# First half of the keys' weights moved to another transfer queue, three short warm-up matmuls removed

## The chip, the cores and the metric

The kernel runs on 1 core of one Trainium2 chip. The time is in device microseconds, from launch to end on that core; lower is better. Before the change it is 173.73 us, the median of 3 runs (173.68 to 174.08).

## The reference: what is computed

A layer norm feeds two branches, whose results are added to the input. Branch A is linear attention: queries, keys and values from one weight matrix, a learned feature map for each of 32 heads (a 16 x 16 matrix, then softmax of the result and of its negative), and a projection. Branch B is a dense layer of width 1792 with the mish activation. All tensors are bf16; S = 2048 tokens, D = 512.

```python
def _A_ref(x, wqkv, w_phi, wo):
    qkv = (x @ wqkv).reshape(B, S, 3, H, Dh).transpose(2, 0, 3, 1, 4)
    q, k, v = qkv[0], qkv[1], qkv[2]
    pq = einsum("bhsd,hdf->bhsf", q, w_phi); pk = einsum("bhsd,hdf->bhsf", k, w_phi)
    phi_q = concatenate([softmax(pq), softmax(-pq)], -1)
    phi_k = concatenate([softmax(pk), softmax(-pk)], -1)
    kv = einsum("bhsf,bhsd->bhfd", phi_k, v); z = einsum("bhsf->bhf", phi_k)
    num = einsum("bhqf,bhfd->bhqd", phi_q, kv)
    den = einsum("bhqf,bhf->bhq", phi_q, z)[..., None] + 1e-6
    return (num / den).transpose(0, 2, 1, 3).reshape(B, S, D) @ wo

def _B_ref(x, w1, b1, w2):
    h = einsum("bsd,df->bsf", x, w1) + b1
    act = h * tanh(softplus(h))
    return einsum("bsf,fd->bsd", act, w2)

xn = layernorm(x)
return x + _A_ref(xn, A_wqkv, A_w_phi, A_wo) + _B_ref(xn, B_w1, B_b1, B_w2)
```

## The kernel before

Tokens are worked on in 16 tiles of 128, four tiles to a group, with the 512 input features in four chunks of 128 rows (kt = 0 to 3). Everything stays in on-chip memory between its load and its last use. The order of the work on every engine is written out by hand: STEPS (line 24) is a list of short step names, each of which issues its instructions when its turn comes, and each engine executes its own instructions in the order in which they were issued. Nothing is reordered later.

The start is what matters here. The feature map's matrix w_phi is folded into the keys' weights once, so that one product of the tokens with the folded weights gives the logits of the keys. For that, the keys' weights (a 512 x 512 block of wqkv) are needed turned. Rows 256 to 511 (kt = 2, 3) are turned by a transposing transfer straight into the tile wT (line 483). Rows 0 to 255 (kt = 0, 1) are loaded as they are into the tile wkp (line 482) and turned on TensorE. The steps in question:

- Warm-ups (line 519): WARM = 9 matmuls of 512 columns and SHORT = 3 of 128 columns on constants, ahead of all else on TensorE. Their results are not used.
- PB (line 537): TensorE transposes the bias b1, loaded by ScalarE's first transfer.
- LS, RS, AZ (lines 165, 171 and 557, 176): layer norm of the first two token tiles: statistics on VectorE, root on GpSimd for tile 0 and on ScalarE for tile 1, application on VectorE.
- TW 0, TW 1 (line 576): TensorE turns rows 0 to 127 and rows 128 to 255 of the keys' weights, four matmuls each. TP 0, TP 1 (line 569): it turns the two token tiles.
- TK 0, TK 1 (line 582): ScalarE copies the turned weights from PSUM into wT.
- WB (line 528): VectorE spreads w_phi (tile wsrc, ScalarE's second transfer, line 488) into the block-diagonal Wbd.
- F0 and FD (lines 151, 160): fold of one chunk on TensorE, and the copy of the folded chunk back into wkp, on ScalarE for chunks 0, 2 and 3, on VectorE for chunk 1. TC (line 588): the copy of a turned token tile.
- LP (line 204): the first logits, eight matmuls. V, H, L (lines 189, 223): values, hidden layer and further logits, which then fill TensorE. M (line 234) is the mish on ScalarE.

Transfers are issued by SyncE, in this order: token tiles 0 and 1, wkp, the transposing load into wT, token tiles 2 and 3, the values' weights wv, the first half of w1, token tiles 4 to 7, the second half of w1, and later ones. ScalarE issues two: b1, then w_phi, both before its first activation table is loaded (line 495). Transfers use eight completion counters in turn; a transfer is issued only when the one that used its counter before has landed.

Of the kernel before, what the change touches and what calls it, by code (L numbers as in the profile page):

```python
# [19 lines left out]

WARM, SHORT = 9, 3
STEPS = """
KM; LS 0; RS 0 p; LS 1; RS 1 a; DX 2; PB @0; AZ 0; AZ 1; TW 0 @1; TW 1 @2; TP 0 @3; TP 1 @4; TK 0 a;
TK 1 a; WB; F0 0 @5; FD 0 a; F0 1 @1; TC 0 v; F0 2 @2; F0 3 @3; FD 2 a; TC 1 v; FD 1 v; FD 3 a; LP i
# [36 lines left out]
def kernel(  # L63
# [12 lines left out]
    nc = tc.nc  # L76
    P = 128
    S, D, NH, DH, F = 2048, 512, 32, 16, 1792
# [10 lines left out]
    wqkv_v = A_wqkv.rearrange("(kt p) c -> p kt c", p=P)  # L89
# [29 lines left out]
    wkp = wts.tile([P, KT, D], BF16, name="wkp")  # L119
# [359 lines left out]


    wT_of = {0: lnp.tile([P, 4, 512], BF16, name="wT", tag="xn")}
    nc.sync.dma_start(wkp[:, 0:2, :], wqkv_v[:, 0:2, D : 2 * D])
    nc.sync.dma_start_transpose(
        out=wT_of[0][:, :, 2 * P : 4 * P], in_=A_wqkv[2 * P : 4 * P, D : 2 * D]
    )
    nc.scalar.dma_start(b1b[:], b1_v[:, :])
    with nc.allow_non_contiguous_dma(reason="tiny w_phi load"):
        nc.scalar.dma_start(wsrc[:], wphi_v)
    nc.sync.dma_start(x_sb[:, 2:4, :], x_v[:, 2:4, :])
    nc.sync.dma_start(wv[:], wqkv_v[:, :, 2 * D : 3 * D])  # L490
    nc.sync.dma_start(w1_sb[:, :, 0 : 7 * P], w1_v[:, :, 0 : 7 * P])
# [189 lines left out]
```

## Time and profile before

| | before |
|---|---|
| median of the runs | 173.73 us |
| the profiled execution | 173.71 us |
| its span, first to last instruction | 172.0 us |
| TensorE (PE) busy | 168.0 us, 98% |
| VectorE (DVE) busy | 143.9 us, 84% |
| ScalarE (ACT) busy | 123.8 us, 72% |
| GpSimd (POOL) busy | 7.8 us, 5% |
| read from HBM, written | 7.10 MB, 2.10 MB |

The profile is that of one execution. Times in it count from the start of the span. PEld is TensorE's weight load, SP is SyncE; a name with a q (SPq, ACTq, PEq) is that engine's sequencer, which issues transfers. In a timeline, a row gives start, duration, engine, line, operation, what is written from what, how many, and in brackets the idle time ahead of it with what ended that. A row of merged instructions gives the whole stretch. The chain of work that ended last is followed back from the last instruction, at each step to what released it. A DMA share over 100% means that packets of one engine overlapped. Line numbers are those of the kernel before.

### The profile page before, as it was taken

The page shows a single profiled execution, that of the slowest core. Times are in us where ns is not written, and L with a number is a line of the kernel's source. Part 1 is how long each engine was busy: PE and PEld are TensorE (multiplying, and loading weights), DVE is VectorE, ACT ScalarE, POOL GpSimd, SP SyncE. Part 2 cuts the span into 40 slices and gives each one's busy share as a digit, 9 for nine tenths or more (in the row PEclk, how much of TensorE's full clock was granted, in tenths as well). Part 3 has the DMA queues.
Part 4 walks back from the last instruction along what each step waited for, and adds up shares of the span by engine and source line. Part 5 has one row for each costly group of instructions (what it writes and reads, how often), then busy time and mean ns, then how long its engine had stood idle before and what let it go on. Part 6 is the DMA issues. An engine that isn't in the chain of part 4 may idle for free.

```text
span 172.0 us, 2735 instructions
## 1 busy us (share of the span) xinstructions
PE 168.0 (98%) x1047; PEld 82.6 (48%) x1047; DVE 143.9 (84%) x223; ACT 123.8 (72%) x199; POOL 7.8 (5%) x23
## 2 busy tenths in 40 slices
PE   8899999999999999999999999999999999999993
PEld 2554444444454544454445644544444444554452
DVE  3869998999599999969989999799799998884333
ACT  2778899997999989889978989977282792432200
POOL 4123002300000000000000000000000000000000
PEclk9999999999999999999999999999999999999999
DMA  4997299589000000000000194309335618668941
GB/s 124 303 370 248 54 255 347 99 162 228 21 0 0 0 4 0 0 0 0 4 0 0 36 113 99 61 9 150 90 97 116 153 52 197 146 134 216 110 131 61
DMA packets 44185, 18.02 MB, mean 105 GB/s; under 512 B 35980, under 2 KB 44172, under 8 KB 44172
## 3 DMA queue, kind: packets, MB, share of 16 engines
q1 hardware_dynamic: 43472, 17.73, 43.9%
q8 instruction: 8, 0.13, 0.4%
q10 hardware_dynamic: 700, 0.12, 0.4%
q14 instruction: 5, 0.04, 0.1%
HBM read 7.10 MB, written 2.10 MB: 53 GB/s over the span
## 4 chain that ended last, share of the span: by engine, by line
PE 95%; DMA 2%; SPq 0%; ACT 0%; issue 0%; DVE 0%
PE po L457 28%; PE ph L223 28%; PE pl L189 14%; PE po L464 8%; PE pv L189 8%; PE pnd L412 2%; PE pkv L381 2%; DMA wkp<-in_A_wqkv_dram 2%; PE pl L204 1%; PE pfold L151 1%; PE pwide L189 1%; SPq L478 0%; PE ptr L569 0%; PE ptw L576 0%; ACT wT L582 0%
## 5 line engine op out<-in xcount | busy, mean ns | idle before, releaser
L457 PE MATMUL po<-w_sb,acts 128*128 128x512 bf16 (+2 forms) x238 | 50.8, 366 | 0.0
L223 PE MATMUL ph<-xnT,w_sb 128*128 128x512 bf16 x224 | 49.8, 379 | 0.0
L234 ACT ACTIVATE acts<-ph,b1f 128x512 bf16<-128x512 f32 x56 | 36.3, 701 | 4.2 <-PE ph L223 4.0
L300 DVE TENSOR_REDUCE s<-e 128x128 f32<-128x2048 bf16 x16 | 36.1, 2276 | 0.5 <-ACT e L283 0.5
L223 PEld LDWEIGHTS <-w_sb 128*128 128x128 bf16 x224 | 21.7, 98 | 25.7
L457 PEld LDWEIGHTS <-acts 128*128 128x128 bf16 x238 | 22.1, 98 | 23.6
L283 ACT ACTIVATE e<-e 128x2048 bf16<-128x2048 bf16 x16 | 30.5, 1919 | 0.0
L189 PEld LDWEIGHTS <-xnT 128*128 128x128 bf16 x184 | 17.5, 98 | 19.6
L471 DVE TENSOR_TENSOR x_sb<-po,x_sb 128x512 bf16<-128x512 f32 (+2 forms) x17 | 11.0, 656 | 8.4 <-PE po L464 8.4
L464 PE MATMUL po<-wqk,xnT 128*128 128x512 bf16 (+2 forms) x68 | 15.6, 366 | 0.0
L189 PE MATMUL pv<-wv,xnT 128*128 128x512 bf16 x64 | 15.6, 379 | 0.0
L189 PE MATMUL pl<-wqk,xnT 128*128 128x512 bf16 x64 | 15.4, 379 | 0.0
L427 ACT COPY ds<-pnd 128x32 f32<-128x32 f32 x16 | 2.9, 182 | 16.5 <-PE pnd L412 16.5
L247 ACT CAST p_sb<-pl 128x512 bf16<-128x512 f32 x21 | 12.2, 594 | 3.6 <-PE pl L189 3.4
L139 ACT ACT_TABLE_LOAD x10 | 12.8, 1283 | 0.2
L258 DVE TENSOR_TENSOR m<-m 128x512 bf16<-128x512 bf16 (+1 forms) x32 | 11.5, 359 | 1.1
L189 PE MATMUL pl<-wkp,xnT 128*128 128x512 bf16 x48 | 11.7, 379 | 0.0
L267 DVE TENSOR_TENSOR e<-p_sb,m 128x2048 bf16<-128x2048 bf16 x8 | 9.8, 1226 | 1.8 <-PE pkv L381 1.5
L258 DVE TENSOR_TENSOR m<-p_sb 128x1024 bf16<-128x1024 bf16 x16 | 10.9, 681 | 0.0
L165 DVE BATCH_NORM_STATS2 stats<-x_sb 128x6 f32<-128x512 bf16 x16 | 10.1, 677 | 0.9 <-DMA x_sb<-in_A_x_dram 0.9
L267 DVE TENSOR_TENSOR e<-m,p_sb 128x2048 bf16<-128x2048 bf16 x8 | 9.8, 1225 | 0.3
L334 DVE TENSOR_TENSOR e<-e,r 128x2048 bf16<-128x2048 bf16 x8 | 9.6, 1216 | 0.5 <-ACT r L309 0.5
(68 smaller groups left out, 133.9 us busy)
## 6 DMA issues: line engine op xcount, KB each, us to landing
w_sb<-in_B_w_dram SPq DMA_DIRECT2D x4, 896.0 KB, 7.8
out_dram<-x_sb SPq DMA_DIRECT2D x15, 128.0 KB, 1.8
x_sb<-in_A_x_dram SPq DMA_DIRECT2D x3, 512.0 KB, 7.5
wv<-in_A_wqkv_dram SPq DMA_DIRECT2D x1, 512.0 KB, 4.6
wqk<-in_A_wo_dram SPq DMA_DIRECT2D x1, 512.0 KB, 4.9
x_sb<-in_A_x_dram SPq DMA_DIRECT2D x2, 128.0 KB, 2.1
wkp<-in_A_wqkv_dram SPq DMA_DIRECT2D x1, 256.0 KB, 3.6
x_sb<-in_A_x_dram SPq DMA_DIRECT2D x1, 256.0 KB, 3.6
```

What stands on the lines that cost most here:

```text
L139: nc.scalar.preload_act_table_set(name)
L189: nc.tensor.matmul(pp, lhsT=xnT[:, t, kt, :], rhs=w[:, kt, :], start=(kt == 0), stop=(kt == KT - 1),)
L223: nc.tensor.matmul(ph_of[u][:], lhsT=w1_sb[:, kt, f * P : (f + 1) * P], rhs=xnT[:, g * TPG : (g + 1) * TPG, kt, :], start=(kt == 0), stop= ...
L234: nc.scalar.activation(acts[:, f, g * 512 : (g + 1) * 512], ph_of.pop(u)[:], ACT.Mish, bias=b1f[:, f : f + 1])
L247: copy(p_of[s][:, i, :], pl_of.pop((s, i)))
L258: nc.vector.tensor_tensor(out=m[:], in0=src[:, :, 0:half], in1=src[:, :, half : 2 * half], op=op)
L267: nc.vector.tensor_tensor(out=e_of[s][:].rearrange("p t j l c -> p (t j) l c")[:, :, pl, :].rearrange("p t (c e o) -> p t c e o", e=8, o=2 ...
L283: nc.scalar.activation(v, v, ACT.Exp)
L300: nc.vector.reduce_sum(t[:], pair(s, k).rearrange("p t j l (c e) -> p (t j l c) e", e=16), axis=AX.X)
L457: nc.tensor.matmul(po_of[t, c.stop][:, c], lhsT=acts[:, f, t * P : (t + 1) * P], rhs=w2_sb[:, f, c], start=(f == 0), stop=False,)
L464: nc.tensor.matmul(po_of[t, c.stop][:, c], lhsT=oT_of[t // 2][:, t % 2 * 4 + j, :], rhs=wo_sb[:, j, c], start=False, stop=(j == 3),)
L471: nc.vector.tensor_tensor(out=y, in0=po_of.pop((t, c.stop))[:, c], in1=y, op=ALU.add)
```

## The change

The load of the keys' weights is split by rows. Rows 128 to 255 (kt = 1) stay with SyncE, at the old place as its third transfer. Rows 0 to 127 (kt = 0) become ScalarE's third transfer, behind b1 and w_phi and ahead of its table load. The three short warm-ups are removed, the nine long ones stay. The steps and their order are the same on every engine, TW 0 ahead of TW 1 included. One transfer more means that from there on each transfer uses the next of the eight completion counters.

```diff
-WARM, SHORT = 9, 3
+WARM, SHORT = 9, 0
...
     wT_of = {0: lnp.tile([P, 4, 512], BF16, name="wT", tag="xn")}
-    nc.sync.dma_start(wkp[:, 0:2, :], wqkv_v[:, 0:2, D : 2 * D])
+    nc.sync.dma_start(wkp[:, 1, :], wqkv_v[:, 1, D : 2 * D])
     nc.sync.dma_start_transpose(
         out=wT_of[0][:, :, 2 * P : 4 * P], in_=A_wqkv[2 * P : 4 * P, D : 2 * D]
     )
     nc.scalar.dma_start(b1b[:], b1_v[:, :])
     with nc.allow_non_contiguous_dma(reason="tiny w_phi load"):
         nc.scalar.dma_start(wsrc[:], wphi_v)
+    nc.scalar.dma_start(wkp[:, 0, :], wqkv_v[:, 0, D : 2 * D])
     nc.sync.dma_start(x_sb[:, 2:4, :], x_v[:, 2:4, :])
```

## The prediction

> **What bounds the kernel now.** I read the busy table first, then the chain of work that ended last, then the first ten microseconds by engine and by queue. The page's busy table and its shares of the chain say which engine sets the end.
>
> ```profile
> PE 168.0 (98%) x1047; PEld 82.6 (48%) x1047; DVE 143.9 (84%) x223; ACT 123.8 (72%) x199; POOL 7.8 (5%) x23
> PE 95%; DMA 2%; SPq 0%; ACT 0%; issue 0%; DVE 0%
> ```
>
> TensorE is busy in 168.0 of 172.0 us. Only 4 us of the span can hold a stall of its own, and the chain's one transfer with 2% is the keys' weights, which the change touches. The stretches show that TensorE doesn't pause again once it has started.
>
> ```profile
> core 0: us, PE busy (x) PEld busy (x) DVE busy (x) ACT busy (x) POOL busy (x), PEclk, DMA share, GB/s
> 9.40:40.00 30.60, 30.60 (x149) 14.13 (x148) 27.53 (x65) 27.97 (x40) 5.26 (x8) 1.00 0.79 213
> ...
> 160.00:168.00 8.00, 8.00 (x43) 3.98 (x42) 2.98 (x5) 0.94 (x3) 0.00 (x0) 1.00 0.44 115
> ```
>
> From 9.4 us to 168 us PE's busy time equals the length of each stretch (the rows left out do too). Whatever moves the work at 9.4 us therefore moves the end by as much; nothing behind it can take up a delay. The question is what the change does before 9.4 us, and the chain of waits of that window answers what sets it.
>
> ```profile
> 1.72 3.59 DMA wkp<-in_A_wqkv_dram
> 5.31 0.05 issue
> 5.36 0.62 PE ptw L576 x8
> 5.98 0.24 PE ptr L569 x4
> 6.22 0.06 issue
> 6.28 0.60 ACT wT L582
> 6.88 0.05 issue
> 6.92 0.84 PE pfold L151 x12
> 7.77 1.79 PE pl L204 x8
> 9.56 0.65 PE pv L189 x3
> ```
>
> Columns are start, duration, what. The load of the first 256 rows of the keys' weights (SyncE's third transfer) lands at 5.31 us. The TW matmuls that turn them start 0.05 us later, ScalarE copies the result (TK), the folds follow, then the first logits, then the full stream. So the first TW at 5.36 us is the hinge: **d**, its shift, is the shift of the end.
>
> **The change part by part.** SyncE's load keeps only rows 128 to 255 (kt = 1); rows 0 to 127 (kt = 0) go out on ScalarE's queue as its third transfer. TensorE's order is kept, so TW 0, which reads kt = 0, still comes first: it waits for the new transfer alone, and behind it in TensorE's queue stand TW 1, the transposes of the tokens and every fold. The half that now lands early gains nothing by itself. These are the issues and ScalarE's work around them.
>
> ```profile
> 1.47 0.41 ACTq L488 DMA_DIRECT2D wsrc<-in_A_w_phi_dram  x1
> 1.91 1.28 ACT L495 ACT_TABLE_LOAD   x1 [1.91 <-issue]
> 4.75 0.29 ACT L557 ACTIVATE rstd<-mv,eps 128x1 f32<-128x1 f32 x1 [1.55 <-DVE mv L167]
> 5.08 0.20 ACT L558 ACTIVATE rstd<-rstd 128x1 f32<-128x1 f32 x1
> 5.79 1.07 ACT L582 CAST wT<-ptw 128x512 bf16<-128x512 f32 x2 [0.51 <-PE ptw L576]
> ```
>
> The added issue on ScalarE takes about 0.41 us, as the one before it does. It runs from 1.9 to 2.3 us and pushes the table load's end from 3.19 to 3.6 us. That is hidden: the next ScalarE work starts at 4.75 us, for another reason, and 1.1 us of idle time is left. Now the landing. The page's table of issues gives the prices, from issue to landing.
>
> ```profile
> x_sb<-in_A_x_dram SPq DMA_DIRECT2D x2, 128.0 KB, 2.1
> wkp<-in_A_wqkv_dram SPq DMA_DIRECT2D x1, 256.0 KB, 3.6
> wsrc<-in_A_w_phi_dram ACTq DMA_DIRECT2D x1, 16.0 KB, 4.0
> ```
>
> A 128 KB load with nothing ahead of it took 2.1 us, so the lower bound of the landing is 1.9 + 2.1 = 4.0 us. But the new load stands behind w_phi, 16 KB in many tiny pieces, which took 4.0 us and landed at 1.47 + 4.0 = 5.47 us, later than the keys' weights. What the queues moved in four stretches (2.8 to 3.4, 3.4 to 4.8, 4.8 to 5.0, 5.0 to 5.3 us; packets, MB, share of 16 engines; q1 is SyncE's queue, q10 ScalarE's) says why.
>
> ```profile
> q1 hardware_dynamic: 44, 0.04, 38.2%
> q10 hardware_dynamic: 169, 0.01, 14.8%
> ...
> DMA packets 965, 0.35 MB, mean 250 GB/s; under 512 B 736, under 2 KB 965, under 8 KB 965
> q1 hardware_dynamic: 657, 0.34, 106.8%
> q10 hardware_dynamic: 308, 0.01, 12.3%
> ...
> q10 hardware_dynamic: 11, 0.00, 3.1%
> ...
> DMA packets 249, 0.06 MB, mean 212 GB/s; under 512 B 249, under 2 KB 249, under 8 KB 249
> q1 hardware_dynamic: 249, 0.06, 103.2%
> ```
>
> ScalarE's queue still moves its last tiny packets at 4.8 to 5.0 us and none after: w_phi is trickled out between SyncE's larger packets. If the queue keeps its order, the new 128 KB begin on each engine when w_phi's packets there are through. At the 250 GB/s of the second stretch 128 KB take 0.52 us: unrelieved, it lands at 5.47 + 0.52 = 5.99 us. Two corrections. SyncE's queue holds 128 KB less ahead of w_phi's later packets, a relief of at most 0.52 us; 308 of ScalarE's packets in these stretches, out of 488, ran beside the keys' load, so I take 308/488 x 0.52 = 0.33 us. Against that, the transposing load of the other weights' rows comes up in SyncE's queue (the 249 packets under 512 B) and takes turns with the new packets. That costs between nothing and 0.52 us (its 256 KB against the new 128 KB, at most byte for byte); I take 0.17 us, about a third, since its packets are the smaller. The landing is then 5.99 - 0.33 + 0.17 = 5.83 us, d = 5.83 - 5.31 = +0.52 us. The bounds behind w_phi are 5.47 us (full relief, no turns) and 6.51 us (no relief, full turns): d = +0.16 to +1.2 us.
>
> The Trainium skill says in DMA: Bandwidth & Descriptors, section Queues, rings and completion order, that each engine consumes a queue's descriptors in ring order, and in the section Issuing engines are not separate DMA queues, that transfers of several issuers interleave on the same 16 engines. Both speak against a gain here; the rows above agree on the interleaving (both queues move in the same stretches), and no row of before shows two large transfers behind each other on ScalarE's queue.
>
> The nine long **warm-ups** stay, the three short ones go.
>
> ```profile
> L514 PEld LDWEIGHTS <-const-bfloat16-1.0 x12: 99/147/147, 0.8 to 4.5; 128*128 128x128 bf16 x12
> L514 PE MATMUL warm<-const-bfloat16-1.0 x12: 221/631/631, 0.8 to 4.6; 128*128 128x512 bf16 x9, 128*128 128x128 bf16 x3
> L576 PE MATMUL ptw<-ident,wkp x8: 219/219/230, 5.4 to 5.8; 128*128 128x128 bf16 x8
> ...
> 0.83 4.00 PE L514 MATMUL warm<-const-bfloat16-1.0 128*128 128x512 bf16 x12 [0.83 <-PEq L665]
> ...
> 4.49 0.34 PE L514 MATMUL warm<-const-bfloat16-1.0 128*128 128x128 bf16 x3
> 4.76 0.18 PE L537 MATMUL pb<-ident,b1b 14*128 14x14 bf16 x1
> ```
>
> Here TensorE's weight loads go from 147 to 99 ns and its short matmuls run at 221 ns, like the TW matmuls behind them (219), so its clock was up before the short ones were through; a long one takes 631 ns before that. The short ones free some 0.2 us ahead of TensorE's wait at 5.36 us, so their removal is worth nothing at the end, and lengthens the pause in front of TW from 0.4 to about 1.2 us.
>
> Also moved: the transfers share eight completion counters in turn, so each issue waits for the transfer eight places before it. With one more transfer, the load of tokens 4 to 7 waits for w_phi instead of the first tokens.
>
> ```profile
> 5.23 0.51 SPq L492 DMA_DIRECT2D x_sb<-in_A_x_dram  x1
> 12.76 2.47 DVE L165 BATCH_NORM_STATS2 stats<-x_sb 128x6 f32<-128x512 bf16 x4 [0.57 <-DMA x_sb<-in_A_x_dram]
> ```
>
> It would issue at 5.5 instead of 5.23 us, in a queue that at 5.0 to 5.3 us is full (103.2% above), with the values' and the hidden layer's weights ahead of it; what hides it is that backlog. Without it VectorE's statistics at 12.76 us would be 0.3 us later, and VectorE isn't on the chain. Cost: nothing. Nothing of it passes POOL's queue.
>
> **Sum**: 0.52 (TW 0 waits for its load) + 0 (issue) + 0 (warm-ups) + 0 (counters). The profiled execution took 173.71 us, span 172.0 and 1.71 around it; the median shown is 173.73. 173.71 + 0.52 = 174.23 us.
>
> **Rivals.** *The relief wins.* Each queue carries 128 KB, both are fed at the same time, and the new load lands at or before 5.3 us. For it: between 2.8 and 3.4 us SyncE's queue used 38.2% of the engines, so there was room. Against it: w_phi's last packets at 4.8 us. The gain has an end: ScalarE's copy at 5.79 us can't start before ScalarE's own root ends (5.08 + 0.20 = 5.28 us), so at most 0.5 us; 0.45 with a hand-over of 0.05. That gives 173.26 to 173.71 us; say 173.5. It is the case that is not slower.
>
> *The transposing load goes first.* If its 256 KB are served wholly ahead of the new load, the latter lands with or after 6.5 us, d = +1.2 us: 174.9 us. It decides once SyncE's queue gets more than a byte for each of ScalarE's. For it: 249 packets in 0.3 us at 103.2% while ScalarE's had ended. Against it: in the second stretch 308 tiny packets came through beside 657.
>
> *TensorE drops back to half clock* in the longer pause. The long warm-ups ran from 0.83 to 4.49 us, 3.66 us, until the clock was up; the same again at half speed costs half of that, 1.8 us: 175.5 us. Against it: the present pause of 0.4 us does no harm, and 1.2 us isn't far from it. In the Trainium skill, TensorE: Matmul & The Clock Gate, section Part 1: The HAM clock gate, half clock returns only after an idle window of about 3.4 us; by that rule this rival costs nothing. No run here shows a pause of that length.
>
> *The change doesn't do what it says*: both halves land together as before, d = 0, 173.71 us; that is the upper end of the first rival.
>
> **How the numbers follow.** Forecast 0.60; relief or no change 0.24; transposing load first 0.10; half clock 0.06. A time within 0.3%, 0.52 us, is about what a measurement of this kernel can't tell from no change, and the forecast lies on that edge (174.25 us). More of its bounds lies above the edge than below, so of its 0.60 I give 0.34 to slower and 0.26 to same: slower 0.34 + 0.10 + 0.06 = 0.50. A gain over 0.3% needs all that the first rival can give and a little more, 0.08 of its 0.24; same keeps 0.26 + 0.16 = 0.42. The likeliest case's own range is 173.87 to 174.91. The range takes in the relief's most and the transposing load's case: 173.35 to 174.95, leaving out the half clock and the ends.
>
> **What would show it.** Right: TW 0 waits for a transfer on ScalarE's queue that ends after w_phi's, the first TW near 5.9 us, kt = 1 in place before that, TW 1 without a wait, everything from the folds to the end shifted alike, the matmuls after the pause still at 219 ns. Wrong: TW 0 at or before 5.36 us (relief); after 6.4 us with the transposing load landed first; ptw matmuls at twice their time (half clock); a new pause of TensorE behind 9.4 us.

## The result, and the profile after

| | before | after |
|---|---|---|
| median of 18 runs each | 173.75 us | 174.41 us |
| lowest to highest | 173.28 to 174.28 us | 173.75 to 175.63 us |
| the profiled execution | 173.71 us | 175.36 us |
| its span | 172.0 us | 173.6 us |

The changed kernel is slower by 0.66 us in the median; the ratio is 1.0044, 95% interval 1.0026 to 1.0063. Its times also spread over 1.9 us instead of 1.0. The execution that was profiled is one of the late ones, 0.95 us above its own median, so its profile holds more than the median's loss.

The chain of waits after the change, its first 12 us (start, duration, what):

```profile
1.46 0.41 ACTq L488
1.87 0.03 issue
1.90 3.73 DMA wkp<-in_A_wqkv_dram
5.64 0.05 issue
5.68 1.03 PE ptw L577 x8
6.72 0.85 PE ptr L570 x8
7.57 1.71 PE pfold L151 x16
9.28 1.66 PE pl L204 x7
10.94 0.04 issue
10.97 1.03 PE pv L189 x4
```

The chain now leaves SyncE's queue and runs over ScalarE's third transfer, which lands at 5.63 us, 0.32 us after the load before. TW starts at 5.68 instead of 5.36 us. But the first value product starts at 10.97 instead of 9.39 us, 1.6 us later. The other 1.3 us lie between TW and that product, and the operations there show what they are (durations in ns, least, median, most; first and last start):

```profile
L515 PE MATMUL warm<-const-bfloat16-1.0 x9: 584/631/631, 0.8 to 4.2; 128*128 128x512 bf16 x9
...
L577 PE MATMUL ptw<-ident,wkp x8: 287/314/314, 5.7 to 6.4; 128*128 128x128 bf16 x8
...
L151 PE MATMUL pfold<-Wbd,wT x16: 314/314/314, 7.4 to 9.0; 128*128 128x128 bf16 x16
...
L204 PE MATMUL pl<-wkp,xnT x7: 379/379/557, 9.1 to 10.5; 128*128 128x512 bf16 x7
```

Before, the TW matmuls took 219 ns; now they take 314, and so do the folds. Only within the first logits, from 557 to 379 ns, does TensorE come to full clock, near 9.3 us. In this execution the nine long warm-ups did not bring it up at all. "Half clock" is worked out from these durations: 384 more columns cost 631 - 314 = 317 ns in the slow state and 379 - 219 = 160 ns in the fast one, about half. The granted clock in the page stays at 9 tenths throughout; the durations show the change, the granted clock doesn't.

The issues and their landings after the change:

```profile
wkp<-in_A_wqkv_dram SPq DMA_DIRECT2D x1, 128.0 KB, 3.7
wkp<-in_A_wqkv_dram ACTq DMA_DIRECT2D x1, 128.0 KB, 3.7
...
wsrc<-in_A_w_phi_dram ACTq DMA_DIRECT2D x1, 16.0 KB, 3.6
```

W_phi lands at 1.46 + 3.6 = 5.06 us (5.47 before), the first half 0.57 us behind it, the second half at 1.72 + 3.7 = 5.42 us.

One sum holds for twelve of the fourteen profiles of this study: the execution's time less the start of the first value product is 164.3 to 164.4 us. It is 173.71 - 9.39 = 164.32 us before and 175.36 - 10.97 = 164.39 after. In those twelve nothing is gained or lost behind that product; it is the clock face on which the experiments are read. The two exceptions, 165.0 and 164.8 us, are the runs with the values' weights issued earlier, where TensorE waits again behind that product.

### The profile page after: what moved, and what is told of

It is laid out like the page before. It is cut to its first block, busy times and chain, and to the rows that moved or that the text cites. A ratio compares the mean times of both kernels' runs of the same rounds, so it can differ in the third digit from the quotient of the medians.

```text
span 173.6 us, 2715 instructions
## 1 busy us (share of the span) xinstructions
PE 168.5 (97%) x1029; PEld 84.0 (48%) x1044; DVE 144.2 (83%) x223; ACT 123.9 (71%) x199; POOL 8.0 (5%) x23
## 4 chain that ended last, share of the span: by engine, by line
PE 95%; DMA 2%; ACTq 1%; issue 1%; DVE 0%
PE ph L223 28%; PE po L457 28%; PE pl L189 14%; PE pv L189 8%; PE po L464 8%; PE pnd L412 2%; PE pkv L381 2%; DMA wkp<-in_A_wqkv_dram 2%; PE pfold L151 1%; PE pwide L189 1%; PE pl L204 1%; PE ptr L570 1%; PE ptw L577 1%; ACTq L486 0%; ACTq L488 0%
```

## The experiments

All were timed in five rounds, 11 or 12 executions each, beside runs of the kernel before on the same chip. "Loss" is the median less that of the kernel before beside it; the ratio, with its 95% interval, stands beside it and is not just the quotient of these two medians, so the two can differ by 0.1 to 0.2 us. Three theories were set against each other at first: A, two terms, a later landing and a later clock; B, the landing alone; C, the clock alone. L stands for a loss made by the keys' half, W for a wait for the values' weights.

**The split alone**, three short warm-ups kept.

```diff
-    nc.sync.dma_start(wkp[:, 0:2, :], wqkv_v[:, 0:2, D : 2 * D])
+    nc.sync.dma_start(wkp[:, 1, :], wqkv_v[:, 1, D : 2 * D])
...
         nc.scalar.dma_start(wsrc[:], wphi_v)
+    nc.scalar.dma_start(wkp[:, 0, :], wqkv_v[:, 0, D : 2 * D])
```

> The split of the load alone: three short warm-ups kept as before. Theory A (two terms: the first half lands about 0.3 us later, and TensorE comes to full clock late in a part of the executions, because the pause ahead of TW 0 became longer): the load lands near 5.6 us in the profile, the end moves by 0.3 us from the landing and by less than the changed kernel from the clock, so 174.0 to 174.3 us. Theory B (all of it is the late landing, the short warm-ups do nothing): the same time as the changed kernel, 174.4 us. Theory C (all of it is the clock): 173.75 to 173.9 us.

Measured: 174.26 us, loss 0.50, ratio 1.0037 (1.0018 to 1.0056). The split without the warm-ups' removal makes most of the loss; C falls. But the profiled execution, the slowest of its twelve with 175.75 us, has a cause that none of the three theories held. TensorE's timeline (start, duration, operation, idle before and what ended it):

```profile
5.37 0.62 PE L577 MATMUL ptw<-ident,wkp 128*128 128x128 bf16 x8
...
7.61 1.95 PE L204 MATMUL pl<-wkp,xnT 128*128 128x512 bf16 x8
11.35 0.82 PE L189 MATMUL pv<-wv,xnT 128*128 128x512 bf16 x3 [1.79 <-DMA wv<-in_A_wqkv_dram]
```

TW is on time (5.37 us), the clock is up, the first logits end as before, and then TensorE waits 1.79 us for the values' weights. Its chain of waits names the transfer:

```profile
4.13 0.05 issue
4.18 7.12 DMA wv<-in_A_wqkv_dram
11.30 0.05 issue
```

7.12 us from issue to landing, where it took 4.6 in the kernel before, though SyncE's queue now held 128 KB less ahead of it.

**The removal of the short warm-ups alone**, load whole.

```diff
-WARM, SHORT = 9, 3
+WARM, SHORT = 9, 0
```

> The removal of the short warm-ups alone: the load of the keys' weights as before. Theory A: the landing stays at 5.3 us and the end moves by the clock alone, about 0.2 to 0.4 us in the median, 173.95 to 174.15 us, with a wider spread of the executions than before. Theory B: 173.75 us, the same as before. Theory C: 174.4 us.

Measured: 173.80 us, loss 0.04, ratio 1.0011 (0.9990 to 1.0033), one of twelve executions at 175.8 us. In the median the short ones are worth nothing that can be measured. In its profile the clock was up in the ninth long one, and it too waited for the values:

```profile
L514 PE MATMUL warm<-const-bfloat16-1.0 x9: 445/631/631, 0.8 to 4.2; 128*128 128x512 bf16 x9
...
4.16 5.58 DMA wv<-in_A_wqkv_dram
9.74 0.05 issue
9.79 1.04 PE pv L189 x4
```

**More short warm-ups**, with the split (eight) and with the load whole (six).

```diff
-WARM, SHORT = 9, 3
+WARM, SHORT = 9, 8
```

> The split, with eight short warm-ups in place of none, so that TensorE is busy until shortly before its load lands near 5.6 us. Theory A: only the landing is left, 0.3 us, so about 174.0 us, with a narrow spread, and in the profile the TW matmuls at 219 ns. Theory B: 174.4 us as the changed kernel. Theory C: 173.75 us or a little less.

> The load as before, with six short warm-ups in place of three, which fill the pause ahead of the TW matmuls to about 5.2 us. Theories A and C: TensorE comes to full clock early in more of the executions, 173.4 to 173.75 us and a narrower spread than before. Theory B: 173.75 us, no change. If the short ones run into the landing at 5.3 us they cost up to 0.1 us.

Measured: 174.38 us, loss 0.62, ratio 1.0036 (1.0020 to 1.0052), with the split; 173.96 us, loss 0.20, ratio 1.0007 (0.9991 to 1.0023), with the load whole. Neither tells the theories apart, because the fill itself came into the way: at half clock a short one takes 312 ns instead of 221, and TW started at 5.73 and 5.52 us, behind its data (the first half had landed at about 1.9 + 3.2 = 5.1 us, the whole load at 1.7 + 3.5 = 5.2 us). Filling a pause by count is no gain where the clock's rise differs between executions.

**The values' weights between token tiles 2 and 3** on SyncE's queue, with the split and with the load whole.

```diff
-    nc.sync.dma_start(x_sb[:, 2:4, :], x_v[:, 2:4, :])
+    nc.sync.dma_start(x_sb[:, 2, :], x_v[:, 2, :])
     nc.sync.dma_start(wv[:], wqkv_v[:, :, 2 * D : 3 * D])
+    nc.sync.dma_start(x_sb[:, 3, :], x_v[:, 3, :])
```

> The split with three short warm-ups, and the values' weights issued by SyncE ahead of the third and the fourth token tile's second half: token tile 2, values' weights, token tile 3. Theory W (the loss of the split is TensorE's wait for the values' weights, whose last engine lands near 9.9 us in three profiles of the split against 8.9 to 9.75 with the load whole, while the first logits end near 9.4): the values land some 0.4 us earlier and the time falls by 0.2 to 0.4 us against 174.26, to 173.9 to 174.05. Theory L (the loss is a late first half of the keys' weights in most executions, the profiles with 5.1 to 5.6 us being the early ones): no change, 174.2 to 174.4 us.

> The control of the run before: the load of the keys' weights whole as before the change, three short warm-ups, and the values' weights between token tiles 2 and 3. Theory W: the wait for the values is small with the load whole, so 173.5 to 173.75 us, a gain of at most 0.2 us. Theory L: 173.75 us, no change. If token tile 3 then lands too late for VectorE, up to 0.3 us slower in both.

Measured: 174.43 us, loss 0.65, ratio 1.0043 (1.0028 to 1.0058), and 173.97 us, loss 0.19, ratio 1.0013 (1.0002 to 1.0024). The expected gain under W did not come. The profile of the first says why the run can't decide: token tile 3 now landed last (9.40 us in its chain, 8.90 with the load whole), VectorE's statistics waited for it, and TensorE for them:

```profile
4.64 4.76 DMA x_sb<-in_A_x_dram
9.40 0.02 issue
9.42 0.71 DVE stats L165
```

The wait was moved, not removed. In both runs, what landed last from SyncE's queue before 10 us was on the path.

**The first half ahead of w_phi** on ScalarE's queue, three short warm-ups.

```diff
+    nc.scalar.dma_start(wkp[:, 0, :], wqkv_v[:, 0, D : 2 * D])
     with nc.allow_non_contiguous_dma(reason="tiny w_phi load"):
         nc.scalar.dma_start(wsrc[:], wphi_v)
-    nc.scalar.dma_start(wkp[:, 0, :], wqkv_v[:, 0, D : 2 * D])
```

> The split with three short warm-ups, and the first half of the keys' weights ahead of w_phi on ScalarE's queue (b1, keys, w_phi) instead of behind it. Theory L, and the prediction's step that the half lands late because it stands behind w_phi: it lands by 4.6 us, w_phi no later than 5.8 us, and the time falls to 173.3 to 173.8 us. Theory W: the landing of the half is early, but the values' weights still land near 9.9 us, so 174.1 to 174.4 us.

Measured: 173.84 us, loss 0.06, ratio 1.0008 (0.9991 to 1.0025). This is the clearest of the runs: the same two halves on the same two queues, and exchanging two transfers on ScalarE's queue takes the loss from 0.50 to 0.06 us. No execution of the split alone was under 173.88 us; nine of the twelve here are at or under it, beside nearly equal medians of the kernel before (173.76 and 173.78 us). Landings, and TensorE:

```profile
wkp<-in_A_wqkv_dram ACTq DMA_DIRECT2D x1, 128.0 KB, 2.6
wkp<-in_A_wqkv_dram SPq DMA_DIRECT2D x1, 128.0 KB, 2.7
wsrc<-in_A_w_phi_dram ACTq DMA_DIRECT2D x1, 16.0 KB, 3.6
...
5.07 0.19 PE L538 MATMUL pb<-ident,b1b 14*128 14x14 bf16 x1
5.19 1.03 PE L577 MATMUL ptw<-ident,wkp 128*128 128x128 bf16 x8
```

The first half takes 2.6 us where it took 3.4 in the run with the split alone, and it is issued 0.43 us earlier (1.48 instead of 1.91 us); how much of the gain each of the two gives was not taken apart. W_phi still lands in time, at 1.87 + 3.6 = 5.47 us. TW no longer waits for data at all: it starts at 5.19 us, right behind the warm-ups and the bias.

**Both halves on SyncE's queue**, ScalarE's queue as before.

```diff
-    nc.sync.dma_start(wkp[:, 0:2, :], wqkv_v[:, 0:2, D : 2 * D])
+    for kt in range(2):
+        nc.sync.dma_start(wkp[:, kt, :], wqkv_v[:, kt, D : 2 * D])
```

> The same two halves, both on SyncE's queue one behind the other (first half, second half), ScalarE's queue as before, three short warm-ups; the completion counters shift as in the changed kernel. If the loss comes from ScalarE's queue (either theory): 173.75 us, keys landing at 5.3 us. If it comes from one transfer more and its counters: 174.2 to 174.4 us.

Measured: 174.08 us, loss 0.30, ratio 1.0010 (0.9993 to 1.0027): between the two expectations, and by its interval not told from no change. In its profile TW starts at 4.50 us, the first logits end near 9.0, and the values' weights stop TensorE:

```profile
4.50 0.40 PE L577 MATMUL ptw<-ident,wkp 128*128 128x128 bf16 x4
5.07 0.40 PE L577 MATMUL ptw<-ident,wkp 128*128 128x128 bf16 x4 [0.18 <-DMA wkp<-in_A_wqkv_dram]
7.30 1.89 PE L204 MATMUL pl<-wkp,xnT 128*128 128x512 bf16 x8
9.65 0.61 PE L189 MATMUL pv<-wv,xnT 128*128 128x512 bf16 x2 [0.47 <-DMA wv<-in_A_wqkv_dram]
```

This kernel has a delay of its own: the second issue on SyncE pushes the values' weights from 4.17 to 4.65 us. So it does not settle whether one transfer more, with its counters, costs something by itself.

**The wait for the values taken away**: the first two value products read the folded keys' weights, all transfers stay. The values of tokens 0 to 255 are then not those of the reference. With the half behind w_phi, with the load whole, and with the half ahead of w_phi.

```diff
-        pv_of[t] = project(wv, t, bank(b, "pv")[:])
+        pv_of[t] = project(wkp if t < 2 else wv, t, bank(b, "pv")[:])
```

> The split with three short warm-ups, but the first two value products read the folded keys' weights in place of the values' weights, so that TensorE doesn't wait for the values' load there; all transfers stay. The values of tokens 0 to 255 are therefore others. Theory W (the split's loss is the wait for the values' weights behind it on SyncE's queue): the loss against the same edit with the load whole shrinks from 0.5 us to 0.1 or less, about 173.6 to 173.8 us; what may be left is a wait for the hidden layer's weights, which come next. Theory L (the loss is made earlier, by the keys' half): 174.2 us, 0.5 us above the whole load.

> The control of the run before: the load whole, three short warm-ups, and the first two value products on the folded keys' weights. The values of tokens 0 to 255 are others. Theory W: the wait for the values is small here, a gain of 0 to 0.15 us, 173.6 to 173.75. Theory L: 173.75 us.

> The last corner of a square: the first half of the keys' weights ahead of w_phi on ScalarE's queue, nine long and three short warm-ups, and the first two value products on the folded keys' weights (the values of tokens 0 to 255 are others). With the half behind w_phi the square has 174.26 us (values awaited) and 174.05 (not awaited), ahead of w_phi 173.84 (awaited). If what is left of the split's loss without the values' wait is the half's place behind w_phi (theory L for that part), this one comes to 173.5 to 173.75 us, some 0.3 to 0.5 below 174.05. If it is made later, by the hidden layer's weights or by the mere split, it stays at 173.95 to 174.1 us. Theory W alone, without L, would want the same 174.05 as behind w_phi.

Losses against the kernel before beside each, with the ratio and its interval:

| the keys' load | values awaited | values not awaited |
|---|---|---|
| whole on SyncE | 0 | -0.18 us, 0.9985 (0.9973 to 0.9998) |
| first half behind w_phi | 0.50 us, 1.0037 (1.0018 to 1.0056) | 0.14 us, 1.0010 (0.9989 to 1.0031) |
| first half ahead of w_phi | 0.06 us, 1.0008 (0.9991 to 1.0025) | -0.13 us, 1.0002 (0.9990 to 1.0014) |

Down each column the place behind w_phi costs: 0.44 us against the place ahead of it with the values awaited, 0.27 us without. Along each row the wait for the values costs: 0.18 us with the load whole, 0.36 behind w_phi, 0.19 ahead of it. Read so, both theories hold a part: W alone would have brought the second row to that of the whole load, and it stays 0.32 us above; L alone would have left it at 0.50. But only the 0.44 us stand clear of the noise, by the spread of the executions given above. The cells were not all measured on one chip; the kernel before itself took 173.91 us beside the first two cells of the right column and 173.72 beside the last, on one and the same chip; and the last cell has a gain of 0.13 us by the medians and a ratio just above one. So the other differences are known to some 0.2 us only. That the place behind w_phi, with the later issue that goes with it, costs time is shown; that the wait for the values has a share in the median is likely, and in single executions it is seen.

**A candidate**: the half ahead of w_phi, eight long warm-ups and three short ones.

```diff
-WARM, SHORT = 9, 3
+WARM, SHORT = 8, 3
```

> A candidate: the first half of the keys' weights ahead of w_phi on ScalarE's queue, eight long and three short warm-ups, so that TensorE is free near 4.6 us when that half lands (4.45 us in the run with nine). Theory W: the first logits end up to 0.4 us earlier, but the values' weights at 9.0 to 9.5 us stop most of it, 173.5 to 173.8 us. Theory L: up to 0.4 us gained, 173.35 us. If eight long ones bring the clock up later in some executions, the upper end of the times rises above 175 us.

Measured: 173.48 us, where the kernel before took 173.91 beside it: 0.43 us less, ratio 0.9982 (0.9964 to 1.0000). Ten of twelve executions lie between 173.39 and 173.74 us; two are at 174.02 and 174.9. TW starts at 4.77, the first value product at 9.01 us:

```profile
4.77 0.96 PE L577 MATMUL ptw<-ident,wkp 128*128 128x128 bf16 x8
...
9.01 1.03 PE L189 MATMUL pv<-wv,xnT 128*128 128x512 bf16 x4
```

It beats the changed kernel, and most likely the kernel before; its interval just touches no change. The 4.45 us of the expectation were the second half's landing in the run with nine long ones (1.70 + 2.7 us); the first half landed there at 1.48 + 2.6 = 4.1 us.

## Why the prediction came out, step by step

The time, 174.41 us against 174.23 forecast, and the direction came out. The steps did so only in part.

*TW 0 waits for a transfer behind w_phi, and this is the loss.* The place was right: the changed kernel's chain runs over ScalarE's queue, the half lands behind w_phi, and moving it ahead of w_phi takes 0.44 us of the loss back. The size was off. The term said a landing at 5.83 us, d = +0.52; the profile has 5.63 us, +0.32. The relief of w_phi was put at 0.33 us and was 0.41 (5.06 instead of 5.47 us); behind w_phi the half was to take 0.52 + 0.17 us and took 0.57. And the other profiles don't show even this d. Here are the landings in us (issue plus time to landing) of what TW 0 waits for, and of w_phi, in five pairs of kernels that match but for the split. In order: no short warm-ups (the changed kernel and the removal alone), three (the split alone and the kernel before), eight and six, three with the values' weights early, three with the values not awaited.

| | half behind w_phi | load whole |
|---|---|---|
| keys' weights | 5.6, 5.3, 5.1, 4.9, 5.3 | 5.4, 5.3, 5.2, 5.0, 5.6 |
| w_phi | 5.1, 4.6, 4.3, 4.4, 4.9 | 5.6, 5.5, 5.3, 5.2, 5.7 |

W_phi landed 0.5 to 1.0 us earlier where the term had 0.33, and the half behind it landed later than the whole load in the first pair alone, by 0.2 us. So the sum's one term, +0.52 us for a late landing, is not what these profiles show. How the place behind w_phi costs the median 0.3 to 0.5 us all the same stays open: only one execution of each kernel is profiled, and in the others the landings are not known.

*Nothing behind 9.4 us takes up or adds a delay, and everything from the folds on shifts alike.* The first half held for this change: time less start of the first value product stayed at 164.3 to 164.4 us. The second failed: in the profile after, TW shifts by 0.32 us and the first value product by 1.58. The clock made that difference there (below). In other kernels a wait that the prediction did not count stands between the two. The values' weights landed at 4.17 + 4.6 = 8.8 us before, 0.6 us ahead of their use. That was the margin of one execution: in the three other profiles with the load whole and the transfers in the same order they took 5.4 to 5.6 us and landed at 9.6 to 9.7 us, 0.2 us or less ahead of the first value product, or behind the time at which it could have started. They were the last to arrive in the profiles of three kernels (9.61, 9.74 and 11.30 us). By the square some 0.2 to 0.4 us of the median's time hangs on them, with the uncertainty said there.

*The short warm-ups are worth nothing at the end.* In the median that is what their removal alone showed (loss 0.04 us). In the profiled execution half clock lasted until 9.3 us, and TW to the first value product took 5.29 us instead of 4.03, 1.26 us more; the sign "matmuls after the pause still at 219 ns" failed, with 314. That is the effect of the third rival, given 0.06, but not its mechanism: TensorE did not drop back in the pause, it had not come up before it (all long warm-ups but the first took 631 ns). That the profiled 175.36 us lie near that rival's 175.5 is chance. Whether the missing short ones cause such executions was not shown. Four of the changed kernel's 18 executions lie above 175.0 us, and none of the 18 of before; one of twelve did with the short ones removed alone. But with three or more short ones kept and a half on ScalarE's queue there are 6 of 84, two of them with the half ahead of w_phi or the values not awaited, and with all keys' weights on SyncE's queue, short ones or not, only 2 of 192. So the late executions go with the half's move to ScalarE's queue more clearly than with the short ones; of the changed kernel's four only one was profiled.

*Issue on ScalarE, counters: nothing.* Right as far as the profile shows. The issue took 0.52 instead of 0.41 us, the table load ended at 3.73 us, and ScalarE's next work came at 4.82. The load of tokens 4 to 7 issued at 5.25 us as before, w_phi having landed by then.

*The rivals.* The relief did not win with the half behind w_phi, and nearly did with it ahead. The transposing load did not go first in the changed kernel: the half lands at 5.63 us, below the 6.5 of that rival. So it was in good part luck that the sum came near the median: its one term was too large for every profiled landing, and part of the loss came from what it left out. Of that, the profiles show the values' wait and the late rise of the clock.

## What to carry to other kernels

Before a transfer is moved to another queue, look at what stands ahead of it there: behind 16 KB in tiny pieces a 128 KB load took 3.0 to 3.7 us in five profiles, ahead of them 2.6 to 3.1 in three, and exchanging the two decided whether the move cost 0.50 or 0.06 us. List with each hidden wait its margin, here for the values' weights 0.6 us in one profile and 0.2 or less in three others; a margin smaller than the spread of landings is part of the path in some executions. And one profile of a kernel whose executions spread by 1 to 2 us shows one way of being late, not the median's.

## What the runs showed of the hardware that was not expected

The moment at which TensorE comes to full clock differs between executions with the same warm-ups. With nine long ones it came by the eighth in one profile and not before the last of the TW matmuls in another:

```profile
L515 PE MATMUL warm<-const-bfloat16-1.0 x12: 218/547/634, 0.8 to 4.2; 128*128 128x512 bf16 x9, 128*128 128x128 bf16 x3
...
L577 PE MATMUL ptw<-ident,wkp x8: 287/314/314, 5.2 to 5.9; 128*128 128x128 bf16 x8
```

The first row is from the run with both halves on SyncE's queue, the second from the one with the half ahead of w_phi. The Trainium skill, TensorE: Matmul & The Clock Gate, section Part 1: The HAM clock gate, says that the window of some 3.4 us on which the clock is decided runs freely and isn't started by the kernel. These profiles agree with that: after the same start at 0.83 us the rise came before 4.2 us in the one, less than one such window after the start, and after 5.9 in the other. By that rule, as an estimate from the 3.4 us, a TensorE that is busy without a pause from 0.83 us on is up after two windows at the latest, at 7.6 us. In every other profile the folds, which start before 7.6 us, run at 219 ns; in the changed kernel, with its pause of 0.7 us before TW, the rise came at 9.3 us. So a pause that falls into the deciding window may cost a further window at half clock without TensorE having been idle for a whole one. That the pause did it here was not shown: one profile alone has such a late rise, and in the one with the short ones removed alone the same pause did no harm, the clock being up before it.

The landing of one and the same transfer also varies. The values' weights, 512 KB, took 4.6, 5.6, 5.4 and 5.4 us from issue to landing in the four profiles with the load whole and the transfers in the order of before (before, short ones removed, six short ones, values not awaited). With both halves on SyncE's queue they took 5.0 us, and with the split alone 7.1, though 128 KB less stood ahead of them.
